# Loading the first x tile by DMA transposes alone, and W1's first blocks from another queue

## The chip, the cores and the metric

The kernel runs on one core of a Trainium2 chip. The metric is the device time of one execution in microseconds (us); lower is better. Times of several executions are given as a median.

## The reference

The kernel computes a gated mix of two branches over a sequence x of 2048 rows and 640 columns, in bf16. Branch a is a state space layer (a linear recurrence with complex coefficients over the rows), branch b is a two-layer perceptron with GELU and 1728 hidden columns.

```
x = A_x
g = sigmoid((x * gate_w).sum(-1, keepdims=True))
# a: S5 layer
dt = exp(log_dt);  Lam_bar = exp(dt * Lam)
B_bar = ((Lam_bar - 1.0) / Lam)[:, None] * Bmat
Bu = einsum("bld,pd->blp", x, B_bar)
h[t] = Lam_bar * h[t-1] + Bu[t]
a = 2.0 * einsum("blp,dp->bld", hseq, Cmat).real + x * Dskip
# b: perceptron
b = gelu(x @ w1 + b1) @ w2 + b2
return g * a + (1 - g) * b
```

## The kernel before

The 2048 rows are worked in four tiles (q = 0 to 3) of 512 rows. The matmuls need x with its columns on the partitions, so each tile is held transposed in `xT[q]`: five slabs (k = 0 to 4) of 128 columns by 512 rows. Most tiles are transposed on the way in by DMA (`xtrans`, a `dma_start_transpose` from DRAM). The first tile is made in two ways. Slabs 0 and 1 are loaded as they lie, in two halves of 256 rows (`xna0`, `xna1`, into `xn[0]`), transposed on TensorE against an identity matrix (L428, four transposes per half), and copied out of PSUM by VectorE (L434). Slabs 2, and 3 and 4, come by two DMA transposes.

The first stage is `m1_first`: the first eight blocks (jf) of 128 hidden columns, for tile 0, one PSUM bank each, summed over the five slabs with the slab as the outer loop, so that each slab and each W1 block (`w1load(k)`, 128 rows of W1 by 1024 columns, 256 KB) is wanted only when its turn comes. In slab 0, six of the eight matmuls are split in two halves of 256 rows, so that the first half can run when only the first half load has come. The matmuls of the last block for slabs 0 and 1 are put off until shortly before it is wanted for slab 2, because its bank (7) is used before that for other things. After `m1_first`, `m1` (L675) works the remaining five blocks of tile 0, bank 0 first, each as one group over the five slabs; bank 0 has to be emptied by ScalarE's first GELU (L662) before that. Then come the projection into the state space (`bproj`, L718), VectorE's recurrence (`ssm`), the second perceptron layer and the output projection.

Ahead of it TensorE runs some matmuls on a constant ("warm", L416) and, between transposes and real matmuls, one filler (L441).

The small vectors (Lambda, log_dt, b1) are loaded as rows of one tile and transposed on TensorE into columns ("cols", L455). VectorE copies them out (L460), and a chain of small steps on ScalarE and VectorE follows: two exponentials, an angle, two sines, each kind with its own ScalarE table load; then the GELU table is loaded, and the GELUs start. VectorE goes on from there to the tables of the recurrence.

The order on each engine is not that of the source. Every operation is given to a list scheduler with an estimated duration, its dependencies and a priority (`prio`); at each step the engine that is free earliest takes its released operation with the lowest priority number. The order so found is emitted as one stream for each engine, with semaphore waits for the dependencies. On SP's stream are most loads; on ScalarE's stream, ahead of all its computing, W1's block 0 and the small rows. TensorE's matmuls are numbered in the order of the source (`pe_prio`), and "cols" has priority 20.5 among them.

Of the kernel before, what the change touches and what calls it, by code (L numbers as in the profile page):

```python
# [147 lines left out]
class Prog:  # L148
# [8 lines left out]
    def op(self, name, eng, dur, reads, writes, fn, prio=None, lat=0.0, after=()):  # L157
        deps = {}
        for k in reads:
            for w in self.last_w.get(k, ()):  # L160
                deps[w.idx] = w
        for k in writes:
            for w in self.last_w.get(k, ()):
                deps[w.idx] = w
            for r in self.last_r.get(k, ()):
                deps[r.idx] = r
        for a in after:
            deps[a.idx] = a
        deps = list(deps.values())
        E = self.E  # L170

        def run(eg, deps=deps, eng=eng, fn=fn):
            E.wait(eng, *[d.done for d in deps if not (eng == "pe" and d.eng == "pe")])
            return fn()

        it = self.sch.add(name, eng, dur, deps, run, prio=prio, lat=lat)
        for k in writes:
            self.last_w[k] = [it]
            self.last_r[k] = []
        for k in reads:  # L180
            self.last_r.setdefault(k, []).append(it)
        return it


def bass_gated_mix__ssm_conv_s5__dense_activation_gelu__prompt_kernel(
# [40 lines left out]
    with ExitStack() as es:  # L226
# [83 lines left out]
        def inc(eng, ins):  # L310
            return E.inc(eng, ins, eng + "_s")

        def dma_inc(eng, ins, sem):
            SEM(sem)
            E.count.setdefault(sem, 0)
            ins.then_inc(sems[sem], 16)
            E.count[sem] += 16
            return (sem, E.count[sem])

        def d_act(n):  # L320
            return 0.26 + n * 0.00084
# [4 lines left out]
        def d_mm(n):  # L326
            return n / 2400.0 + 0.004


        def load(name, eng, sem, dst, src, writes, prio, dur=0.5, lat=2.5, reads=(), after=()):  # L330
            def fn():
                with nc.allow_non_contiguous_dma(reason="columns of small vectors"):
                    return dma_inc(eng, engines[eng].dma_start(dst, src), sem)
            return op(name, eng, dur, reads, writes, fn, prio=prio, lat=lat, after=after)

        def load_T(name, sem, pairs, writes, prio, dur, lat=3.0, reads=()):
            def fn():
                t = None
                for dst, src in pairs:
                    t = dma_inc("sp", nc.sync.dma_start_transpose(dst, src), sem)  # L340
                return t
            return op(name, "sp", dur, reads, writes, fn, prio=prio, lat=lat)

        def xnload(q, eng, prio=None):
            load(f"xn{q}", eng, f"l_xn{q}", xn[q % 2][:, :, :],
# [4 lines left out]
        FW = NW * 128  # L350
        nmain = (NF - 1) * 128

        def xtrans(q, ks, prio, dur):
            load_T(f"xT{q}_{ks[0]}", f"l_xT{q}_{ks[0]}", [(xT[q][:, ks[0]:ks[-1] + 1, :], x2[q * 512:(q + 1) * 512, ks[0] * 128:(ks[-1] + 1) * 128])],
                   [("xT", q, k) for k in ks], prio, dur)

        WSPLIT = {}

# [5 lines left out]
        def w1tok(k, jf):  # L364
            return ("w1", k, int(jf >= WSPLIT.get(k, NW)))

        KN = 2

        for h in range(2):
            load(f"xna{h}", "sp", f"l_xna{h}", xn[0][:, 2 * h:2 * h + 2, 0:KN * 128],  # L370
                 x2[h * 256:(h + 1) * 256, 0:KN * 128].rearrange("(c p) d -> p c d", p=128), [("xna", h)], 0.2 * h, dur=0.45, lat=2.0 + 0.4 * h)
        w1load(1, "sp", 1)
        w1load(2, "sp", 4)
        xtrans(0, range(2, 3), 5, 1.15)
        w1load(3, "sp", 6)
        xtrans(0, range(3, 5), 7, 1.8)
        w1load(4, "sp", 8)
# [8 lines left out]
            return inc("pool", nc.gpsimd.memset(rows[:, :], 0.0))  # L386

        op("rz", "pool", 0.2, (), list(ROWS) + [("b1b", 0), ("b1b", 1), "rz"], f_rz, prio=-90)
        w1load(0, "act", -110, reads=["rz"])
        for i, (nm, (r0, src)) in enumerate(ROWS.items()):  # L390
            src = src.rearrange("(k p) -> k p", p=128)
            load(nm, "act", "l_" + nm, rows[r0:r0 + src.shape[0], :], src, [nm], prio=-100 + i, dur=0.4)
# [19 lines left out]

        def f_warm():
            t = None
            for n in (512,) * 5 + (384,):
                t = nc.tensor.matmul(PS[4][:, 0:n], one.broadcast_to([128, 128]), one.broadcast_to([128, n]), start=True, stop=True)  # L416
            return inc("pe", t)

        op("warm", "pe", 2.7, (), [("bank", 4)], f_warm, prio=-1000)

        for i, (k, c0, c1) in enumerate(((0, 0, 2), (1, 0, 2), (0, 2, 4), (1, 2, 4))):
            bank = (7, 6, 7, 6)[i]
            pt = PS[bank][:, :].bitcast(BF16)[:, 0:(c1 - c0) * 128]

            def f_xt(k=k, pt=pt, c0=c0, c1=c1):
                t = None
                for c in range(c0, c1):
                    t = nc.tensor.transpose(pt[:, (c - c0) * 128:(c - c0 + 1) * 128], xn[0][:, c, k * 128:(k + 1) * 128], ident[:, :])  # L428
                return inc("pe", t)

            op(f"xt{i}", "pe", 0.11 * (c1 - c0), [("xna", c0 // 2), "ident"], [("bank", bank)], f_xt, prio=-990 + i if i < 2 else 3.1 + 0.1 * i)

            def f_xc(k=k, pt=pt, c0=c0, c1=c1):
                return inc("dve", nc.vector.tensor_copy(out=xT[0][:, k, c0 * 128:c1 * 128], in_=pt))  # L434

            op(f"xc{i}", "dve", 0.42, [("bank", bank)], [("xT", 0, k, c0)], f_xc, prio=-2000 + i)

        def f_fill():
            t = None
            for _ in range(1):  # L440
                t = nc.tensor.matmul(PS[3][:, 0:256], one.broadcast_to([128, 128]), one.broadcast_to([128, 256]), start=True, stop=True)  # L441
            return inc("pe", t)

        op("fill", "pe", 0.11, [("xna", 0), "ident"], [("bank", 3)], f_fill, prio=-900)

        XK0 = [[("xT", 0, k)] for k in range(KD)]
        XK0[0] = [("xT", 0, 0, 0), ("xT", 0, 0, 2)]
        XK0[1] = [("xT", 0, 1, 0), ("xT", 0, 1, 2)]
        XT = {q: [("xT", q, k) for k in range(KD)] for q in range(1, NQ)}
        XT[0] = [t for x in XK0 for t in x]  # L450

        psC = PS[7][:, :].bitcast(BF16)[:, 0:128]

        def f_cols():
            return inc("pe", nc.tensor.transpose(psC, rows[:, :], ident[:, :]))  # L455

        op("cols", "pe", 0.3, list(ROWS) + [("b1b", 0), ("b1b", 1), "ident"], [("bank", 7)], f_cols, prio=20.5)

        def f_cols1():
            return inc("dve", nc.vector.tensor_copy(out=cols[:, :], in_=psC[:, 0:RT + 1]))  # L460
# [128 lines left out]
        for ci, src in enumerate((A_B_re, A_B_im)):  # L589
            for i, (p0, p1) in enumerate(((0, 512), (512, KP * 128))):  # L590
                load_T(f"B{ci}{i}", f"l_B{ci}{i}", [(BT[:, ci, :, p0:p1], src[p0:p1, :])], [("BT", ci, i)], prio=30 + ci + 0.1 * i, dur=0.8 * (p1 - p0) / 128)
        xtrans(1, range(KD), 32, 3.4)
        load("gwb", "sp", "l_gwb", gwb[:, :], gate_w.partition_broadcast(128), ["gwb"], prio=32.2)
        load("xnb", "sp", "l_xnb", xn[0][:, :, KN * 128:D], x2[0:512, KN * 128:D].rearrange("(c p) d -> p c d", p=128),
             [("xn", 0, 0), ("xn", 0, 1)], 32.4, dur=1.0, lat=6.0, reads=[("xna", 0), ("xna", 1)])
        big = load("w2a", "sp", "l_w2a", W2sb[:, 0:NF - 1, :], B_w2[0:nmain, :].rearrange("(j p) d -> p j d", p=128), ["w2a"], prio=33, lat=8.0)
        load("w2b", "sp", "l_w2b", W2sb[0:FL, NF - 1, :], B_w2[nmain:F, :], ["w2b"], prio=34, lat=4.0)
        load("w2c", "sp", "l_w2c", W2sb[64:64 + FL, NF - 1, :], B_w2[nmain:F, :], ["w2c"], prio=34.2, lat=4.0)
# [42 lines left out]


        def m1_first():
            late = [(0, NW - 1), (1, NW - 1)]
            seq = [(k, jf) for k in range(KD) for jf in range(NW) if (k, jf) not in late]
            i = seq.index((2, NW - 1))
            seq[i:i] = late
            steps = [(0, jf, h) for h in range(2) for jf in range(6)] + [(k, jf, None) for k, jf in seq if k or jf > 5]
            for k, jf, h in steps:
                t0, t1 = (0, 512) if h is None else (256 * h, 256 * h + 256)  # L650

                def f_mm(jf=jf, k=k, t0=t0, t1=t1):
                    return inc("pe", nc.tensor.matmul(PS[jf][:, t0:t1], W1sb[:, k, jf * 128:(jf + 1) * 128], xT[0][:, k, t0:t1],  # L653
                                                      start=(k == 0 and t0 == 0), stop=(k == KD - 1), skip_group_check=jf < 6))

                op(f"m1_0_{jf}_{k}_{t0}", "pe", d_mm(t1 - t0), (XK0[k] if h is None else XK0[k][h:h + 1]) + [w1tok(k, jf)], [("bank", jf)],
                   f_mm, prio=pe_prio())
            for jf in range(NW):
                ctr["bank"] += 1

                def f_ge(jf=jf):
                    return inc("act", nc.scalar.activation(Gl[0][:, jf, :], PS[jf][:, :], ACT.Gelu_apprx_tanh, bias=b1col[:, jf:jf + 1]))  # L662

                op(f"ge_0_{jf}", "act", d_act(512), [("bank", jf), "b1col"], [("gl", 0, jf)], f_ge, prio=10)
# [344 lines left out]
        def outsT(q, mid=None):  # L1009
# [58 lines left out]
            for d in range(KD):  # L1068

                def f_dx(d=d):  # L1070
                    for _ in range(14 if q == NQ - 2 else 0):
                        nc.scalar.nop(nofuse=True)
                    return inc("act", nc.scalar.activation(xT[q][:, d, :], xT[q][:, d, :], ACT.Copy, scale=cols2[:, 1, d:d + 1]))  # L1073

                op(f"dx_{q}_{d}", "act", d_act(512), [("cols2", 1)], XK0[d] if q == 0 else [("xT", q, d)], f_dx, prio=20)

            for d in range(KD):
                bank = next_bank()
# [123 lines left out]
```

## Time and profile before

| | us |
|---|---|
| median of 3 runs | 212.66 (212.58 to 212.69) |
| the profiled execution | 211.84 |
| its span in the profile | 210.5 |
| TensorE busy | 206.9 (98%) |
| VectorE busy | 191.0 (91%) |
| ScalarE busy | 102.7 (49%) |

The profiled execution's time is 1.34 us more than its span, which counts from the first to the last event of the core. In the timeline a line gives the start, the time from the first start to the last end of the instructions merged in it, the engine, the line of the kernel and the operation; "SPq" and "ACTq" are the issues of transfers from those engines' streams. A transfer's time to landing is counted from its issue. PEld are TensorE's weight loads, which overlap its matmuls. Matmuls overlap one another in the records: a 512-column matmul is recorded as 379 ns long while the next starts earlier.

### The profile page before, as it was taken

Reading aid. Unit: us, or ns where it says so; the run is one execution under the profiler, and the core shown is the slowest. Engines: PE = TensorE matmul, PEld = TensorE weight load, DVE = VectorE, ACT = ScalarE, POOL = GpSimd, SP = SyncE. Lnnn points to the kernel's source line nnn. Section 1 sums busy time; section 2 is a strip of 40 time slices with the busy share of each in tenths; the row PEclk is TensorE's granted clock in tenths of the full one; section 3 lists DMA queues with packets and bytes.
Section 4 is the critical chain, followed back from the end, with each engine's and each line's share of the span. In section 5 each row is a group of like instructions: output and inputs, shape, how many; then the busy total and the mean of one; then the engine's idle time right before and its main releaser. Section 6 shows DMA issues by size and latency. Waiting matters only on the chain.

```text
span 210.5 us, 2557 instructions
## 1 busy us (share of the span) xinstructions
PE 206.9 (98%) x987; PEld 95.1 (45%) x1004; DVE 191.0 (91%) x244; ACT 102.7 (49%) x166; POOL 4.2 (2%) x12
## 2 busy tenths in 40 slices
PE   8999999999999999999999999999999999999996
PEld 4544444444444444444444444444444444444444
DVE  2499999999999999999999999899999999899482
ACT  2398556679850533556683222455664253204321
POOL 1000000030000000000000000000010000000000
DMA  6999999999500020053373000006631000006623
GB/s 191 271 230 124 200 204 226 361 190 207 129 0 4 0 50 0 0 107 65 80 61 113 3 0 0 0 2 140 142 87 58 0 0 4 0 2 145 135 71 100
DMA packets 50248, 19.47 MB, mean 93 GB/s; under 512 B 43068, under 2 KB 48828, under 8 KB 50236
## 3 DMA queue, kind: packets, MB, share of 16 engines
q1 hardware_dynamic: 47904, 17.59, 38.2%
q0 software_dynamic: 1600, 1.32, 4.3%
q10 hardware_dynamic: 732, 0.40, 0.7%
q8 instruction: 8, 0.13, 0.3%
q14 instruction: 4, 0.03, 0.1%
HBM read 8.68 MB, written 2.63 MB: 54 GB/s over the span
## 4 chain that ended last, share of the span: by engine, by line
PE 98%; issue 0%; DVE 0%
PE ps L675 22%; PE ps L718 20%; PE ps L1015 20%; PE ps L1085 15%; PE ps L809 5%; PE ps L653 4%; PE ps L922 4%; PE ps L829 1%; PE ps L416 1%; PE ps L696 1%; PE ps L882 1%; PE ps L1050 1%; PE ps L428 0%; PE ps L846 0%; DVE W1sb L954 0%
## 5 line engine op out<-in xcount | busy, mean ns | idle before, releaser
L675 PE MATMUL ps<-xT,W1sb 128*128 128x512 bf16 x214 | 47.5, 379 | 0.3
L762 DVE TENSOR_TENSOR_SCAN W<-atab,V 128x1280 bf16<-128x1280 f32 x16 | 44.3, 2812 | 0.3
L718 PE MATMUL ps<-xT,BT 128*128 128x512 bf16 x196 | 43.3, 379 | 0.2
L1015 PE MATMUL ps<-Gl,W2sb 128*128 128x512 bf16 x192 | 42.8, 379 | 0.2
L682 ACT ACTIVATE Gl<-ps,cols 128x512 bf16<-128x512 f32 x44 | 29.8, 695 | 15.5 <-PE ps L675 15.5
L675 PEld LDWEIGHTS ps<-xT,W1sb 128*128 128x128 bf16 x220 | 21.5, 98 | 26.0
L1085 PE MATMUL ps<-Hb,CT 128*128 128x512 bf16 x150 | 32.9, 379 | 0.0
L729 ACT ACTIVATE U<-ps 128x512 bf16<-128x512 f32 x40 | 23.7, 596 | 15.5 <-PE ps L718 15.5
L718 PEld LDWEIGHTS ps<-xT,BT 128*128 128x128 bf16 x200 | 19.4, 98 | 23.8 <-ACT Gt L704 0.4
L1015 PEld LDWEIGHTS ps<-Gl,W2sb 128*128 128x128 bf16 x195 | 18.9, 98 | 23.3 <-issue 0.7
L1023 ACT ACTIVATE E1T<-ps,cols 128x512 bf16<-128x512 f32 x15 | 10.0, 686 | 26.2 <-PE ps L1015 14.7
L1085 PEld LDWEIGHTS ps<-Hb,CT 128*128 128x128 bf16 x150 | 14.7, 98 | 17.7
L1093 ACT ACTIVATE E2T<-ps 128x512 bf16<-128x512 f32 x15 | 9.0, 597 | 21.7 <-PE ps L1085 21.7
L627 DVE SCALAR_TENSOR_TENSOR trf<-xn,gwb 128x640 bf16<-128x640 bf16 x16 | 13.2, 823 | 0.4
L505 DVE TENSOR_TENSOR V<-V,W 128x1280 bf16<-128x1280 bf16 x16 | 12.5, 821 | 0.3
L505 DVE TENSOR_TENSOR Hb<-Hb,V 128x1280 bf16<-128x1280 bf16 x16 | 12.5, 821 | 0.3
L505 DVE TENSOR_TENSOR V<-mr,U 128x2560 bf16<-128x2560 bf16 x8 | 11.9, 1492 | 0.3
L505 DVE TENSOR_TENSOR Hb<-c,W 128x2560 bf16<-128x2560 bf16 x8 | 11.9, 1490 | 0.2
L809 PE MATMUL ps<-W2sb,Gl 128*128 128x512 bf16 x51 | 11.8, 379 | 0.1
L505 DVE TENSOR_TENSOR V<-s,W 128x2560 bf16<-128x2560 bf16 x8 | 11.9, 1484 | 0.0
L505 DVE TENSOR_TENSOR W<-mi,U 128x2560 bf16<-128x2560 bf16 x8 | 11.9, 1483 | 0.0
L1073 ACT ACTIVATE xT<-xT,cols 128x512 bf16<-128x512 bf16 x15 | 10.0, 712 | 0.0
(103 smaller groups left out, 148.2 us busy)
## 6 DMA issues: line engine op xcount, KB each, us to landing
W2sb<-in_B_w_dram SPq DMA_DIRECT2D x1, 2080.0 KB, 8.4
out_dram<-xn SPq DMA_DIRECT2D x3, 640.0 KB, 5.5
xn<-in_A_x_dram POOLq DMA_DIRECT2D x2, 640.0 KB, 7.0
W1sb<-in_B_w_dram SPq DMA_DIRECT2D x4, 256.0 KB, 4.0
trf<-grow SPq DMA_DIRECT2D x4, 256.0 KB, 4.9
xn<-in_A_x_dram SPq DMA_DIRECT2D x1, 640.0 KB, 7.2
W1sb<-in_B_w_dram SPq DMA_DIRECT2D x1, 480.0 KB, 5.6
W1sb<-in_B_w_dram SPq DMA_DIRECT2D x1, 400.0 KB, 6.4
```

Of the source, the lines that this page charges most:

```text
L505: return inc("dve", nc.vector.tensor_tensor(out=o, in0=a, in1=b, op=o_))
L627: t = inc("dve", nc.vector.scalar_tensor_tensor(out=scr[:, :], in0=xn[q % 2][:, c, :], scalar=1.0, in1=gwb[:, :], op0=ALU.mult, op1=ALU.mu ...
L675: t = nc.tensor.matmul(PS[bank][:, :], W1sb[:, k, jf * 128:(jf + 1) * 128], xT[q][:, k, :], start=(k == 0), stop=(k == KD - 1))
L682: return inc("act", nc.scalar.activation(Gl[q % 2][:, jf, :], PS[bank][:, :], ACT.Gelu_apprx_tanh, bias=b1col[:, jf:jf + 1]))
L718: t = nc.tensor.matmul(PS[bank][:, :], BT[:, ci, kd, k * 128:(k + 1) * 128], xT[q][:, kd, :], start=(kd == 0), stop=(kd == KD - 1))
L729: return inc("act", nc.scalar.activation(dst, src, ACT.Copy, scale=1.0 if ci == 0 else -1.0))
L762: t = inc("dve", nc.vector.tensor_tensor_scan(out=g[:, ci, :], data0=a, data1=v[:, ci, :], initial=0.0, op0=ALU.mult, op1=ALU.add))
L809: t = nc.tensor.matmul(PS[bank][:, :], Gl[q % 2][:, jf, t4 * 128:(t4 + 1) * 128], W2sb[:, jf, 0:DN], start=False, stop=False, skip_group_c ...
L1015: t = nc.tensor.matmul(PS[bank][:, :], W2sb[:, jf, d * 128:(d + 1) * 128], Gl[q % 2][:, jf, :], start=(jf == 0 and not lead), stop=(jf == ...
L1023: return inc("act", nc.scalar.activation(E1T[:, d, :], PS[bank][:, :], ACT.Identity, bias=cols2[:, 0, d:d + 1]))
L1073: return inc("act", nc.scalar.activation(xT[q][:, d, :], xT[q][:, d, :], ACT.Copy, scale=cols2[:, 1, d:d + 1]))
L1085: t = nc.tensor.matmul(PS[bank][:, :].rearrange("p (s t) -> p s t", s=2), CT[:, ci, k, d * 128:(d + 1) * 128], Hb[:, 2 * (q % 2):2 * (q % ...
```

## The change

The two half loads, the eight TensorE transposes, VectorE's four copies, the filler and the splitting of matmuls go. Slab 0, and slabs 1 and 2, come by two DMA transposes that are the first two transfers of SP's stream. W1's blocks 0, 1 and 2 are issued at the head of ScalarE's stream, without waiting for the clearing of the rows tile, in place of one there and two on SP's. One more constant matmul of 512 columns is in the warming. The priority of "cols" goes from 20.5 to 18.5. Later, `xn[0]` is loaded whole (640 KB) in place of the three slabs that were missing (384 KB).

```
-        KN = 2
-
-        for h in range(2):
-            load(f"xna{h}", "sp", f"l_xna{h}", xn[0][:, 2 * h:2 * h + 2, 0:KN * 128],
-                 x2[h * 256:(h + 1) * 256, 0:KN * 128].rearrange("(c p) d -> p c d", p=128), [("xna", h)], 0.2 * h, dur=0.45, lat=2.0 + 0.4 * h)
-        w1load(1, "sp", 1)
-        w1load(2, "sp", 4)
-        xtrans(0, range(2, 3), 5, 1.15)
+        xtrans(0, range(0, 1), 0, 1.2)
+        xtrans(0, range(1, 3), 1, 1.2)
         w1load(3, "sp", 6)
         xtrans(0, range(3, 5), 7, 1.8)
         w1load(4, "sp", 8)
...
-        w1load(0, "act", -110, reads=["rz"])
+        w1load(0, "act", -110)
+        w1load(1, "act", -109)
+        w1load(2, "act", -108)
...
-            for n in (512,) * 5 + (384,):
+            for n in (512,) * 6 + (384,):
...
-        for i, (k, c0, c1) in enumerate(((0, 0, 2), (1, 0, 2), (0, 2, 4), (1, 2, 4))):
...
-        op("fill", "pe", 0.11, [("xna", 0), "ident"], [("bank", 3)], f_fill, prio=-900)
...
-        op("cols", "pe", 0.3, list(ROWS) + [("b1b", 0), ("b1b", 1), "ident"], [("bank", 7)], f_cols, prio=20.5)
+        op("cols", "pe", 0.3, list(ROWS) + [("b1b", 0), ("b1b", 1), "ident"], [("bank", 7)], f_cols, prio=18.5)
...
-        load("xnb", "sp", "l_xnb", xn[0][:, :, KN * 128:D], x2[0:512, KN * 128:D].rearrange("(c p) d -> p c d", p=128),
-             [("xn", 0, 0), ("xn", 0, 1)], 32.4, dur=1.0, lat=6.0, reads=[("xna", 0), ("xna", 1)])
+        xnload(0, "sp", 32.4)
...
-            late = [(0, NW - 1), (1, NW - 1)]
-            seq = [(k, jf) for k in range(KD) for jf in range(NW) if (k, jf) not in late]
+            seq = [(k, jf) for k in range(KD) for jf in range(NW) if k > 1 or jf < NW - 1]
             i = seq.index((2, NW - 1))
-            seq[i:i] = late
-            steps = [(0, jf, h) for h in range(2) for jf in range(6)] + [(k, jf, None) for k, jf in seq if k or jf > 5]
-            for k, jf, h in steps:
-                t0, t1 = (0, 512) if h is None else (256 * h, 256 * h + 256)
-
-                def f_mm(jf=jf, k=k, t0=t0, t1=t1):
-                    return inc("pe", nc.tensor.matmul(PS[jf][:, t0:t1], W1sb[:, k, jf * 128:(jf + 1) * 128], xT[0][:, k, t0:t1],
-                                                      start=(k == 0 and t0 == 0), stop=(k == KD - 1), skip_group_check=jf < 6))
-
-                op(f"m1_0_{jf}_{k}_{t0}", "pe", d_mm(t1 - t0), (XK0[k] if h is None else XK0[k][h:h + 1]) + [w1tok(k, jf)], [("bank", jf)],
-                   f_mm, prio=pe_prio())
+            seq[i:i] = [(0, NW - 1), (1, NW - 1)]
+            for k, jf in seq:
+
+                def f_mm(jf=jf, k=k):
+                    return inc("pe", nc.tensor.matmul(PS[jf][:, :], W1sb[:, k, jf * 128:(jf + 1) * 128], xT[0][:, k, :],
+                                                      start=(k == 0), stop=(k == KD - 1)))
+
+                op(f"m1_0_{jf}_{k}", "pe", d_mm(512), [("xT", 0, k), w1tok(k, jf)], [("bank", jf)], f_mm, prio=pe_prio())
```

More of the change, by code (lines that the diff above doesn't have):

```diff
@@ L334, in load, with load_T @@
             return op(name, eng, dur, reads, writes, fn, prio=prio, lat=lat, after=after)
-        def load_T(name, sem, pairs, writes, prio, dur, lat=3.0, reads=()):
+        def load_T(name, sem, pairs, writes, prio, dur, lat=3.0, reads=(), eng="sp"):
             def fn():
@@ L339, in fn @@
                 for dst, src in pairs:
-                    t = dma_inc("sp", nc.sync.dma_start_transpose(dst, src), sem)
+                    t = dma_inc(eng, engines[eng].dma_start_transpose(dst, src), sem)
                 return t
-            return op(name, "sp", dur, reads, writes, fn, prio=prio, lat=lat)
+            return op(name, eng, dur, reads, writes, fn, prio=prio, lat=lat)
         def xnload(q, eng, prio=None):
@@ L351, in bass_gated_mix__ssm_conv_s5__dense_activation_gelu__prompt_kernel, with xtrans @@
         nmain = (NF - 1) * 128
-        def xtrans(q, ks, prio, dur):
+        def xtrans(q, ks, prio, dur, eng="sp"):
             load_T(f"xT{q}_{ks[0]}", f"l_xT{q}_{ks[0]}", [(xT[q][:, ks[0]:ks[-1] + 1, :], x2[q * 512:(q + 1) * 512, ks[0] * 128:(ks[-1] + 1) * 128])],
-                   [("xT", q, k) for k in ks], prio, dur)
+                   [("xT", q, k) for k in ks], prio, dur, eng=eng)
         WSPLIT = {}
@@ L419, in bass_gated_mix__ssm_conv_s5__dense_activation_gelu__prompt_kernel @@
         op("warm", "pe", 2.7, (), [("bank", 4)], f_warm, prio=-1000)
-        for i, (k, c0, c1) in enumerate(((0, 0, 2), (1, 0, 2), (0, 2, 4), (1, 2, 4))):
[L422 to L442, printed above, removed]
-        op("fill", "pe", 0.11, [("xna", 0), "ident"], [("bank", 3)], f_fill, prio=-900)
[L446 to L450, printed above, removed]
+        XT = {q: [("xT", q, k) for k in range(KD)] for q in range(NQ)}
         psC = PS[7][:, :].bitcast(BF16)[:, 0:128]
@@ L1073, in f_dx @@
                     return inc("act", nc.scalar.activation(xT[q][:, d, :], xT[q][:, d, :], ACT.Copy, scale=cols2[:, 1, d:d + 1]))
-                op(f"dx_{q}_{d}", "act", d_act(512), [("cols2", 1)], XK0[d] if q == 0 else [("xT", q, d)], f_dx, prio=20)
+                op(f"dx_{q}_{d}", "act", d_act(512), [("cols2", 1)], [("xT", q, d)], f_dx, prio=20)
             for d in range(KD):
```

## The prediction

> **What bounds the kernel now.** I read the page first: engine shares and the chain that ended last.
>
> ```profile
> PE 206.9 (98%) x987; PEld 95.1 (45%) x1004; DVE 191.0 (91%) x244; ACT 102.7 (49%) x166; POOL 4.2 (2%) x12
> PE 98%; issue 0%; DVE 0%
> ```
>
> TensorE is busy nearly all the span and the chain never leaves it. A change at the start is therefore worth what it does to the moment at which TensorE falls into its unbroken stream: all later work slides with it. So I read TensorE's timeline at the start, then the queues' (start, length, what):
>
> ```profile
> 0.78 2.61 PE L416 MATMUL ps<-const-bfloat16-1.0 128*128 128x512 bf16 x6 [0.78 <-PEq L1187]
> 3.19 0.63 PE L428 MATMUL ps<-ident,xn 128*128 128x128 bf16 x4
> 3.61 0.42 PE L441 MATMUL ps<-const-bfloat16-1.0 128*128 128x256 bf16 x1
> 3.99 0.72 PE L653 MATMUL ps<-xT,W1sb 128*128 128x256 bf16 x3
> 4.55 0.39 PE L428 MATMUL ps<-ident,xn 128*128 128x128 bf16 x4
> 4.77 2.99 PE L653 MATMUL ps<-xT,W1sb 128*128 128x256 bf16 x17
> 7.60 0.22 PE L455 MATMUL ps<-ident,rows 128*128 128x128 bf16 x1
> 7.66 5.78 PE L653 MATMUL ps<-xT,W1sb 128*128 128x512 bf16 x25
> 13.27 1.03 PE L675 MATMUL ps<-xT,W1sb 128*128 128x512 bf16 x4
> ...
> 2.74 1.20 SPq L340 DMA_TRANSPOSE xT<-in_A_x_dram  x1
> 4.61 1.25 SPq L340 DMA_TRANSPOSE xT<-in_A_x_dram  x1
> ```
>
> The stream's rate: 25 L675 matmuls run from 13.27 to 18.66, 0.2155 us each. The 40 full matmuls of the first tile take 8.62 us of it, and the transpose of the small rows ("cols", L455) 0.055. Counted back from 13.27, an unbroken stream would have started at **4.60**. The first real matmul is at 3.99, but waits and 8 transposes in between use up the lead. 4.60 is the number to beat.
>
> **What is removed.** Two loads of half of x's first two slabs, 8 TensorE transposes, one filler, 4 VectorE copies, and the splitting of 6 matmuls into 12. All of TensorE's part lies before the stream closes up, so its whole worth is in the 4.60. The copies (0.3 us each) go from an engine that idles 2.4 us just ahead of them: nothing more. An added 512-column warming matmul (0.43 us apart in the trace there) ends the warming at 0.78 + 6 x 0.427 + 0.32 = 3.66, before any data can be there: nothing.
>
> **When the first matmul can start.** It needs slab 0 and W1's block 0. Block 0, now without the wait for the memset, is issued at 0.74 instead of 0.97; its 2.8 us to landing give 3.54. A DMA transpose of one slab from DRAM landed 4.2 us after issue (queued behind 512 KB of W1); one of the same size between SBUF tiles, late in the kernel with idle queues, 2.4:
>
> ```profile
> DMA to landing us min/median/max: 4.2/4.2/4.3
> ...
> DMA to landing us min/median/max: 2.4/2.4/2.4
> ```
>
> (the first answer is for xT in the first 14 us, the second for the transpose into Gl). So slab 0 lands between 0.74 + 2.4 = 3.14 and 0.74 + 4.2 = 4.94. It has an empty queue of its own but three W1 blocks beside it; I take 4.3 (estimate, a little above the middle). Seven matmuls, one of them still at the slow clock, end at about 6.0.
>
> **When the second slab is there.** Block k=1 now waits for the two-slab transpose, issued right behind the first at 0.74 + 1.20 = 1.95. Nearest row: the two-slab transpose of before, 4.3 us, which gives 6.25. Bytes say the same: slab 0, slabs 1 and 2 and W1's three blocks are 1152 KB, exactly what before had moved (half loads, three blocks, slab 2) between the first packet at 1.8 and the last at about 6.25, semaphore at 6.94. My first packets are at about 2.0 (an ACT load showed its own 1.3 us after issue), so at the same pace the last lands at 7.1; were the pieces to run one after the other at their own best rates (about 350 GB/s for W1, 288 for transposes in the trace), at 2.0 + 3.6 + 0.7 = 6.3. Shortest: 3.6 us, the small second B_re transpose, gives 5.6. I take 6.35 and a start of k=1 at 6.4, bounds 5.65 to 7.15. An unbroken stream from 4.60 would start k=1 at 4.60 + 7 x 0.2155 = 6.10. **Term 1: +0.3 us** (-0.45 to +1.05).
>
> The W1 blocks take 0.40 us of issue each on ScalarE's queue; queued behind them are the six loads of the small rows, last issue about 4.1 instead of 3.57, wanted only past 8.5, and ScalarE's first table load, wanted past 9. The Trainium skill ("DMA: Bandwidth & Descriptors", section "Issuing engines are not separate DMA queues") says that transfers from several issuers share the same 16 engines and that spreading them saves issue time only. By that rule, 7.1 stands before 6.3. The trace agrees as far as it goes: while both queues had work (2.2 to 3.6) the total stayed at 290 to 420 GB/s, near one queue's own.
>
> **What the order does to GELU.** This is a wait that the diff hides. "cols" feeds the chain to the first GELU:
>
> ```profile
> 7.86 0.19 DVE L460 CAST cols<-ps 128x29 f32<-128x29 bf16 x1 [2.51 <-PE ps L455]
> 8.82 1.28 ACT L498 ACT_TABLE_LOAD   x1
> 10.76 1.28 ACT L662 ACT_TABLE_LOAD   x1
> 12.06 1.84 ACT L662 ACTIVATE Gl<-ps,cols 128x512 bf16<-128x512 f32 x3
> ```
>
> It is a serial chain: 4.46 us from cols (7.60) to GELU (12.06), 0.69 for the first one, bank 0 free at 12.75. TensorE wants bank 0 at 13.27: 0.52 us of slack. In the order of before, cols stands behind work equal to 14 full matmuls; in the new order (priority 18.5) it stands behind 18. Four matmuls are 0.86 us, so the slack turns into 0.52 - 0.86 = -0.34, plus a semaphore: **term 2: +0.4 us** (0.3 to 0.5; zero only if some later wait on TensorE, say for slabs 3 and 4, holds it anyway). Later banks come free every 0.6 us and are wanted every 1.08, so only the first waits.
>
> **What is moved or grows, at no cost.** W1's block 3 and all behind it on SP's queue are issued about 0.75 us earlier (transposes 1.20 + 1.25 in place of 0.97 + 0.94 + 1.20, and the block): slabs 3 and 4 at 3.85, plus 4.3, land at 8.15, wanted at about 10; the rest of W1 was there at 12.3 and 13.6 for 13.3 and 16.5. The full x load in place of the 384 KB one adds 256 KB, 0.9 us at 290 GB/s, ahead of two x transposes and W2; W2 would land at about 42.7 instead of 41.8 and is first used at 56.66. VectorE's long chain starts relative to TensorE 0.86 - 0.4, about 0.5 us later; the first matmul on its result runs at 71.77, the result is complete at 67.94; at the end VectorE idles 2.7 us at once. Without those covers each would cost its own size.
>
> **Sum.** +0.3 + 0.4 = +0.7 us. The profiled execution is 211.84 (span 210.5 and 1.34 around it), which becomes 212.55; the median of the runs is 212.66, 0.82 more, so I add the same 0.7 to it: **213.4 us**. A change within 0.2%, 0.43 us, can't be told from none here.
>
> **Rivals.**
> (a) The forecast, about 212.9 to 213.9: chance 0.5.
> (b) Not slower: transposes at the head of an empty queue go through nearly as the 2.4 us row. The first matmul starts at 3.6 as W1 allows, one or two run at the slow clock, and k=1 starts at its lower bound 5.65: -0.45, and with cols' wait about -0.05, 212.6. It decides where slabs 1 and 2 land before 5.6. Over 0.43 us faster it is only if the GELU wait is covered too, at 212.2. For it: nothing stands ahead of them. Against: 768 KB of W1 ask the same engines at the same moment, and every DRAM transpose shown took 3.6 or more. Chance 0.25, of that 0.1 clearly faster.
> (c) The transposes get the engines last: 7.1, term 1 is +1.0, sum +1.4, 214.1. For it: from 2.6 to 3.2 of the trace ScalarE's block took nearly all packets while SP's second half load waited. Chance 0.13.
> (d) The clock. Until about 4.4 TensorE runs at half rate: weight loads last 147 ns before and 98 after, 512-column matmuls stand 427 ns apart and later 215.5, though the page's granted clock reads 1.00 throughout. It rises some 3.6 us after the first matmul, having seen near-unbroken work. Now TensorE idles from 3.66 to 4.3. If that delays the rise to 7 or later, seven matmuls take 3.0 us, k=1 starts at 7.3 and some of its own are slow: about +1.1 over the forecast, 214.5. Against: the new warming is 2.88 us of real matmuls, as much as before had without counting transposes. Chance 0.12. The Trainium skill ("TensorE: Matmul & The Clock Gate", Part 1) says the clock is released after a sustained busy window of about 3.4 us, free-running; the rise at 4.4 fits that, and whether 0.6 us idle breaks it no run here shows.
> That the change would not do what it says is out: in the new order the two transposes are SP's first two and the blocks ScalarE's first three, with no wait ahead.
>
> **Range and chances.** 212.4 to 214.6 takes in (b) to (d) but for their ends. Slower by over 0.2% holds (c), (d) and most of (a): 0.65; same 0.24; faster 0.11.
>
> **What would show it.** Right: first real matmul at 4.0 to 4.6, a gap on TensorE ahead of k=1 until about 6.4, released by the DMA into xT, a second gap of 0.3 to 0.5 ahead of the first L637 matmul (the old L675), released by ScalarE's GELU, that matmul at about 14.0. Wrong: no gap at k=1 (b), weight loads of 147 ns past 5 (d), no wait on GELU, or a new TensorE gap anywhere after 20 us.

## The result and the profile after

The changed kernel takes 215.26 us (median of 4 runs, 214.1 to 215.59), the kernel before 212.62 us in the same comparison (4 runs). The ratio is 1.0119, 95% interval 1.0077 to 1.016: about 2.5 us slower, where 0.7 was forecast, and above the stated range. The profiled execution of after took 215.59 us; its span is 214.3, 3.8 longer than that of before.

TensorE's timeline and the queues' at the start of the changed kernel, as shown for before:

```profile
0.74 1.36 ACTq L333 DMA_DIRECT2D W1sb<-in_B_w_dram  x3
0.74 2.56 SPq L340 DMA_TRANSPOSE xT<-in_A_x_dram  x2
...
0.78 3.04 PE L412 MATMUL ps<-const-bfloat16-1.0 128*128 128x512 bf16 x7 [0.78 <-PEq L1149]
5.43 6.21 PE L616 MATMUL ps<-xT,W1sb 128*128 128x512 bf16 x18 [1.61 <-DMA xT<-in_A_x_dram]
11.48 0.22 PE L422 MATMUL ps<-ident,rows 128*128 128x128 bf16 x1
11.53 4.91 PE L616 MATMUL ps<-xT,W1sb 128*128 128x512 bf16 x22
16.77 5.56 PE L637 MATMUL ps<-xT,W1sb 128*128 128x512 bf16 x25 [0.33 <-ACT Gl L624]
```

TensorE idles for 1.61 us until slab 0 lands, its first real matmul is at 5.43 instead of 3.99, and the first L637 matmul (L675 of before) is at 16.77 instead of 13.27: +3.50. From there on the two timelines keep that distance (the first L680 matmul, L718 of before, at 22.16 against 18.66; the last transfers' issue at 211.95 against 208.45). So all of the loss but 0.3 us sits ahead of 16.8 us; the 0.3 comes behind the issue of the last stores. The part ahead of 16.8 us has three pieces that can be read here.

The two transposes' times to landing (first slab 0, then slabs 1 and 2):

```profile
DMA to landing us min/median/max: 4.6/4.6/4.6
...
DMA to landing us min/median/max: 5.7/5.7/5.7
```

They land at 5.34 and about 7.7. The weight loads, one for each matmul, show the clock. First two of the kernel before, then those of L616 in the changed one:

```profile
4.39 0.15 PEld L428 LDWEIGHTS ps<-ident,xn 128*128 128x128 bf16 x1
6.09 0.10 PEld L653 LDWEIGHTS ps<-xT,W1sb 128*128 128x128 bf16 x1
...
5.83 0.15 PEld L616 LDWEIGHTS ps<-xT,W1sb 128*128 128x128 bf16 x1 [0.28 <-issue]
7.96 0.15 PEld L616 LDWEIGHTS ps<-xT,W1sb 128*128 128x128 bf16 x1 [0.28 <-DMA xT<-in_A_x_dram]
9.67 0.15 PEld L616 LDWEIGHTS ps<-xT,W1sb 128*128 128x128 bf16 x1 [0.28 <-issue]
9.97 1.18 PEld L616 LDWEIGHTS ps<-xT,W1sb 128*128 128x128 bf16 x6
```

In the changed kernel they last 147 ns and stand 0.43 us apart until just before 9.97; in the trace of before those of 147 ns end at 4.4. The 18 matmuls from 5.43 to 11.48 take 6.05 us, where at 0.2155 us each they would take 3.88: the slow clock costs 2.17 us. The wait for GELU costs more than the 0.33 us shown: the 22 matmuls behind "cols" start at 11.53 and would, at 0.2155 us each, let L637 start at 16.27, so the stream loses 0.50. (The idle time shown counts from the recorded end of the last matmul, and a matmul recorded as 379 ns long ends 0.16 us after the next could have started.) An unbroken full-speed stream from 5.43 would reach L637 at 5.43 + 8.675 = 14.1; with 2.17 for the clock and 0.50 for GELU this is 16.77, all of it. Against before, the 3.50 us are thus 0.83 for the later start (5.43 against 4.60), 2.17 and 0.50.

There is no gap ahead of k=1: slabs 1 and 2 land at 7.7, and the seven slow matmuls of k=0 end only at about 8.4. So the parts overlap: at full clock TensorE would have stood waiting for slabs 1 and 2 until 7.7. What each is worth alone is a matter for runs.

### The profile page after: what moved, and what is told of

Same layout as the page of the kernel before. It is cut to its first block, busy times and chain, and to the rows that moved or that the text cites. A ratio compares the mean times of both kernels' runs of the same rounds, so it can differ in the third digit from the quotient of the medians.

```text
span 214.3 us, 2540 instructions
## 1 busy us (share of the span) xinstructions
PE 209.4 (98%) x990; PEld 94.3 (44%) x990; DVE 190.0 (89%) x240; ACT 102.7 (48%) x166; POOL 4.2 (2%) x12
## 4 chain that ended last, share of the span: by engine, by line
PE 94%; DMA 2%; ACT 1%; DVE 1%; issue 0%
PE ps L637 22%; PE ps L680 20%; PE ps L977 20%; PE ps L1047 15%; PE ps L771 5%; PE ps L884 4%; PE ps L616 3%; DMA xT<-in_A_x_dram 2%; PE ps L791 1%; PE ps L658 1%; PE ps L844 1%; PE ps L1012 1%; ACT L624 1%; ACT Gl L624 0%; PE ps L808 0%
## 5 line engine op out<-in xcount | busy, mean ns | idle before, releaser
L637 PE MATMUL ps<-xT,W1sb 128*128 128x512 bf16 x220 | 48.1, 379 | 0.3 <-ACT Gl L624 0.3
L680 PE MATMUL ps<-xT,BT 128*128 128x512 bf16 x200 | 43.8, 379 | 0.0
L637 PEld LDWEIGHTS ps<-xT,W1sb 128*128 128x128 bf16 x220 | 21.4, 98 | 26.5 <-issue 0.8
L680 PEld LDWEIGHTS ps<-xT,BT 128*128 128x128 bf16 x200 | 19.4, 98 | 23.8 <-ACT Gt L666 0.4
L616 PE MATMUL ps<-xT,W1sb 128*128 128x512 bf16 x40 | 11.0, 443 | 1.6 <-DMA xT<-in_A_x_dram 1.6
```

The source lines that it names most:

```text
L616: return inc("pe", nc.tensor.matmul(PS[jf][:, :], W1sb[:, k, jf * 128:(jf + 1) * 128], xT[0][:, k, :], start=(k == 0), stop=(k == KD - 1)))
L637: t = nc.tensor.matmul(PS[bank][:, :], W1sb[:, k, jf * 128:(jf + 1) * 128], xT[q][:, k, :], start=(k == 0), stop=(k == KD - 1))
L680: t = nc.tensor.matmul(PS[bank][:, :], BT[:, ci, kd, k * 128:(k + 1) * 128], xT[q][:, kd, :], start=(kd == 0), stop=(kd == KD - 1))
```

## The experiments

Each kernel was timed against the kernel before on the same chip; its median was 212.1 to 212.3 us in these comparisons. Differences in us are worked out from the ratios, which take in all runs of a kernel and can differ by some tenths of a us from the difference of two medians. The kernel before ran at 211.76 to 212.78 us in these comparisons, and its profile is of a run of 211.84, near the fast end; differences between two profiles can therefore be larger than those between all runs.

**A busy TensorE until the data come** (`e1_warm`, on the changed kernel):

```
-            for n in (512,) * 6 + (384,):
+            for n in (512,) * 11 + (384,):
```

> The changed kernel with 11 instead of 6 warming matmuls of 512 columns, so that TensorE has no idle time before slab 0 lands at about 5.4. Theory (the idle time from 3.8 to 5.4 broke the busy stretch that the clock needs): slow weight loads (147 ns) end by about 5 instead of 10, the seven matmuls of k=0 run at 0.2155 us, k=1 then waits for slabs 1 and 2 at about 7.75, and the first L637 matmul comes at 7.75 + 33 x 0.2155 + 0.055 + 0.33 = 15.25 instead of 16.77: about 1.5 us less, 213.7. Rival (the loss is the late landing of the transposes, the slow clock only fills time that would be waited anyway): under 0.3 us less than the changed kernel, about 215.

Measured: 214.06 us, ratio to before 1.0081 (1.0063 to 1.0098). TensorE's timeline:

```profile
0.78 4.53 PE L412 MATMUL ps<-const-bfloat16-1.0 128*128 128x512 bf16 x12 [0.78 <-PEq L1149]
5.24 1.68 PE L616 MATMUL ps<-xT,W1sb 128*128 128x512 bf16 x7
7.91 2.55 PE L616 MATMUL ps<-xT,W1sb 128*128 128x512 bf16 x11 [0.99 <-DMA xT<-in_A_x_dram]
...
15.59 2.75 PE L637 MATMUL ps<-xT,W1sb 128*128 128x512 bf16 x12 [0.32 <-ACT Gl L624]
```

The slow weight loads end at 4.55, the seven matmuls of k=0 take 1.68 us instead of 3, and then TensorE waits for slabs 1 and 2 until 7.91. L637 comes at 15.59, 1.2 us sooner than in after. The idle stretch thus kept the clock low; its net price is 1.2 us in the profiles and, between the two ratios, 0.4% or 0.8 us. The two ratios' intervals overlap (1.0077 to 1.016 and 1.0063 to 1.0098), so the 0.8 is rough. What is left, 1.7 us, is not the clock.

**The clock alone** (`e2_before_idle`, on the kernel before; no transfer is touched):

```
-            for n in (512,) * 5 + (384,):
+            for n in (512,) * 2:
```

> The kernel before with only 2 warming matmuls of 512 columns; no transfer is touched. TensorE idles from about 1.8 to 3.2. Theory (clock): the rise moves from about 4.4 to between 7 and 10.5, some 6 to 14 matmuls run at 0.427 instead of 0.2155 us: 1.3 to 3 us slower, 214 to 215.6. Rival (clock not tied to idle time, or covered by the waits for slabs): within 0.3 us of 212.6.

Measured: 213.05 us, ratio 1.0044 (1.0028 to 1.0061); L675 at 14.74 instead of 13.27. TensorE sits idle for 1.26 us (to 3.05), slow weight loads go on to 7.8 instead of 4.4. The direction is the theory's and the rival is out. The loss is 1.5 us in the profiles; by the ratio it is 0.9, under the expected 1.3 to 3, and the rise, at 7.8, came at the early end of what was expected.

**The GELU wait alone** (`e3_before_cols`, on the kernel before):

```
-        op("cols", ..., [("bank", 7)], f_cols, prio=20.5)
+        op("cols", ..., [("bank", 7)], f_cols, prio=24.5)
```

> The kernel before with the transpose of the small rows four full matmuls later (priority 24.5), nothing else. Theory (the 0.52 us of slack ahead of the first GELU turn into a wait of 0.34 us plus a semaphore): a TensorE wait of 0.3 to 0.4 us ahead of the first L675 matmul, released by GELU, 213.0. Rival (the chain to GELU is covered): no wait, 212.6.

Measured: 212.53 us, ratio 1.0022 (1.001 to 1.0034), 0.5 us. The wait is there, of the size worked out, and as in after it costs the stream more than is shown (22 matmuls from 8.66 would end in a start at 13.40; L675 comes at 13.89, 0.49 later):

```profile
8.61 0.22 PE L455 MATMUL ps<-ident,rows 128*128 128x128 bf16 x1
8.66 4.91 PE L653 MATMUL ps<-xT,W1sb 128*128 128x512 bf16 x21
13.89 4.48 PE L675 MATMUL ps<-xT,W1sb 128*128 128x512 bf16 x20 [0.32 <-ACT Gl L662]
```

**Both taken out of the changed kernel** (`e4_warm_cols`): 11 warming matmuls as in `e1_warm`, and

```
-        op("cols", ..., [("bank", 7)], f_cols, prio=18.5)
+        op("cols", ..., [("bank", 7)], f_cols, prio=14.5)
```

> The changed kernel with 11 warming matmuls (as e1_warm) and the transpose of the small rows after 14 instead of 18 matmuls (priority 14.5). Theory: the wait of 0.32 us for the first GELU goes, and nothing takes its place: first L637 matmul at about 15.25 instead of 15.6, 0.3 us under e1_warm. Rival (another wait, for slabs 3 and 4 or for the small rows, is late next): no gain over e1_warm.

Measured: 213.05 us, ratio 1.0039 (1.0026 to 1.0053). No wait on GELU is left and L637 comes at 14.69:

```profile
7.50 1.69 PE L616 MATMUL ps<-xT,W1sb 128*128 128x512 bf16 x7 [0.47 <-DMA xT<-in_A_x_dram]
```

The step from `e1_warm` is 0.9 us in the profiles: the GELU wait cost the stream of `e1_warm` 0.49, and in this execution slabs 1 and 2 also landed 0.4 us sooner (k=1 at 7.50). What is left against before, 0.8 us by the ratio and 1.42 in the profiles, is the late data: k=1 starts 1.40 us after the 6.10 of an unbroken stream.

**W1's blocks back on SP's queue** (`e5_w1_sp`, on the changed kernel):

```
         xtrans(0, range(0, 1), 0, 1.2)
+        w1load(1, "sp", 0.5)
         xtrans(0, range(1, 3), 1, 1.2)
+        w1load(2, "sp", 4)
...
-        w1load(1, "act", -109)
-        w1load(2, "act", -108)
```

(The planner's assumed latencies of the loads that are moved or stand next to them are lowered as well, so that TensorE's order stays that of after; these arguments are left out of the lines shown here, and in `e7_mix` and `e8_behind`.)

> The changed kernel with W1's blocks 1 and 2 back on SP's queue, block 1 behind the first transpose and block 2 behind the second; block 0 stays on ScalarE's. Theory (slab 0's data had passed by 3.6, and only its last small packets, the completion, stood behind the W1 blocks of ScalarE's queue until 5.3): slab 0 lands at 0.74 + 3.5 = about 4.3, TensorE's first real matmul at 4.3 to 4.5. Rival (a transpose from DRAM at the head of the queue takes 4.6 whatever runs beside it): first matmul at 5.4 again. Time by the theory 213 to 214.3, since slabs 1 and 2 are issued 0.5 later; by the rival 215 or more.

Measured: 213.54 us, ratio 1.0087 (1.0054 to 1.0119); four of its six runs are at 213.4 to 213.6, two at 215.2 and 215.3. Slab 0 lands after 3.6 instead of 4.6 us, slabs 1 and 2 after 4.1 instead of 5.7:

```profile
4.38 2.22 PE L616 MATMUL ps<-xT,W1sb 128*128 128x512 bf16 x7 [0.56 <-DMA xT<-in_A_x_dram]
6.77 1.68 PE L616 MATMUL ps<-xT,W1sb 128*128 128x512 bf16 x7 [0.17 <-DMA xT<-in_A_x_dram]
8.74 1.04 PE L616 MATMUL ps<-xT,W1sb 128*128 128x512 bf16 x4 [0.28 <-DMA W1sb<-in_B_w_dram]
```

The rival, that a DRAM transpose at the head takes 4.6 whatever runs beside it, is out. The packets of the queues in the trace of after (q1 is SP's, q10 ScalarE's; packets, MB, share), first for 2.6 to 3.6 us, then for 3.6 to 4.8, show where the microsecond was:

```profile
q1 hardware_dynamic: 512, 0.13, 57.4%
q10 hardware_dynamic: 102, 0.18, 50.2%
...
q10 hardware_dynamic: 183, 0.34, 106.5%
q1 hardware_dynamic: 34, 0.00, 1.7%
```

Slab 0's 512 rows had all moved by 3.6. In the next 1.2 us SP's queue moved only 34 packets of next to no bytes, among 0.34 MB of ScalarE's queue, and the semaphore came at 5.34. That the 34 are slab 0's completion is an inference; that the W1 blocks on the other queue made it late, the runs show: slab 0 takes 4.6, 4.5 and 4.6 us in the three kernels with all three blocks ahead there (after, `e1_warm`, `e4_warm_cols`) and 3.5 to 4.0 in the four others on the changed kernel.

**That part of the change alone** (`e6_before_act`, on the kernel before):

```
-        w1load(1, "sp", 1)
-        w1load(2, "sp", 4)
...
         w1load(0, "act", -110, reads=["rz"])
+        w1load(1, "act", -109, reads=["rz"])
+        w1load(2, "act", -108, reads=["rz"])
```

> The kernel before with W1's blocks 1 and 2 on ScalarE's queue behind block 0 instead of SP's; nothing else. Theory (transfers from SP complete late when W1 blocks wait on the other queue): the second half load lands at 5 or later instead of 4.1, TensorE waits for it, the first L675 matmul comes 0.5 to 1 us later, 212.6 to 213.1. Rival (the bytes are the same, the place does not matter, and slab 2 is issued 1 us earlier): the same as before or up to 0.2 us less.

Measured: 214.27 us, ratio 1.0097 (1.0082 to 1.0111), 2.1 us. The move of two W1 blocks to the other queue, with nothing else, costs nearly as much as the whole change, above the expected 212.6 to 213.1. The place was not the one expected:

```profile
4.62 3.00 PE L653 MATMUL ps<-xT,W1sb 128*128 128x256 bf16 x17
9.68 0.22 PE L455 MATMUL ps<-ident,rows 128*128 128x128 bf16 x1 [2.06 <-DMA rows<-in_B_b_dram]
9.84 7.46 PE L653 MATMUL ps<-xT,W1sb 128*128 128x512 bf16 x25
17.13 1.24 PE L675 MATMUL ps<-xT,W1sb 128*128 128x512 bf16 x5
```

The second half load landed after 3.1 us instead of 2.9, no matter. Late were the small rows, now behind the two blocks on ScalarE's queue, for which TensorE stood 2.06 us, and slab 2, which took 6.5 us from issue instead of 4.2. Slab 2 was there at 8.3, before the rows, so only the rows held TensorE up; the changed kernel has no such wait, and this run prices the move of the blocks in the kernel before, not their share of the change. After the idle time the clock fell, and here the granted clock shows it (after the engines' busy times: granted clock, DMA share, GB/s):

```profile
10.50:13.80 3.30, 3.30 (x9) 1.17 (x8) 3.08 (x10) 3.02 (x5) 0.00 (x0) 0.50 1.20 323
```

(This profile is the longest of its runs, 215.7; the others were 213.7 to 214.4, which the wait of 2.06 us would account for without the slow matmuls.)

**Only block 1 beside the second transpose** (`e7_mix`, on the changed kernel): 8 warming matmuls, "cols" at 14.5, and

```
         xtrans(0, range(1, 3), 1, 1.2)
+        w1load(2, "sp", 4)
...
-        w1load(1, "act", -109)
-        w1load(2, "act", -108)
+        w1load(1, "act", -98.5)
```

> The changed kernel with W1's block 1 on ScalarE's queue only after two of the small rows, block 2 on SP's behind the two transposes, 8 warming matmuls and the small rows' transpose after 14 matmuls. Theory: slab 0 lands at about 4.4, slabs 1 and 2 at 6.0 to 6.7, no GELU wait, full clock by about 5: the first L637 matmul at 13.3 to 14.0, so 212.1 to 212.9, level with before (212.1 in the last comparison) or up to 0.8 behind. Rival (transposes at the head of the stream always cost some 2 us): 214.

Measured: 213.32 us, ratio 1.0051 (1.0039 to 1.0064). Slab 0 lands after 3.5 us as expected; slabs 1 and 2 take 5.2, k=1 starts at 7.25 and L637 comes at 14.45, so the time is above the expected 212.1 to 212.9. One block on the other queue is enough to hold the second transpose up.

**No further block beside it** (`e8_behind`, on the changed kernel): 8 warming matmuls, "cols" as in after, and blocks 1 and 2 both on SP's queue behind the two transposes:

```
         xtrans(0, range(1, 3), 1, 1.2)
+        w1load(1, "sp", 4)
+        w1load(2, "sp", 5)
...
-        w1load(1, "act", -109)
-        w1load(2, "act", -108)
```

> The changed kernel with W1's blocks 1 and 2 on SP's queue behind both transposes, and 8 warming matmuls. Theory (the second transpose is slow because W1 blocks of the other queue are in flight with it): slabs 1 and 2 land about 4.2 us after issue, near 6.2, instead of 5.4 to 5.8 after; W1's block 1 is then the late one, near 7.3. Rival (behind another transpose from DRAM, a two-slab transpose takes over 5 us by itself): landing at 7.2 or later, with nothing beside it. Time by both near 213.3: the landing decides.

Measured: 213.91 us, ratio 1.0073 (1.0047 to 1.0099). The second transpose's time to landing:

```profile
DMA to landing us min/median/max: 3.7/3.7/3.7
```

3.7 instead of 5.4 to 5.8, so slabs 1 and 2 are there at 5.7, before the 6.10 of an unbroken stream. The rival is out. But now W1's block 1 is late (k=1 at 7.51, released by its load): the same bytes have to come before k=1 in whatever order. They are 896 KB (slabs 0 to 2 and two blocks); the kernel before needs 768 KB for its k=1 (two half loads and two blocks). A transfer of slab 1 alone was not tried.

Are slabs 1 and 2 late because of the queue, or of the bytes alone? With 640 KB issued up to and with them (`e8_behind`) they land at 5.7; with 896 KB at 6.75 and 6.95 where the block stands ahead on SP's own queue (`e5_w1_sp`, `e9_sp_warm`) and at 7.2 where it is on the other one (`e7_mix`); with 1152 KB at 7.45 to 7.9. So, as far as single profiles can tell, most of it goes with the bytes, and for one block 0.25 to 0.45 us with the queue. But the bytes do not pass at an even pace. In the stretch ahead of these landings little moved in after and `e1_warm` (first after, then `e1_warm`; the last column is GB/s):

```profile
5.60:6.40 0.80, 0.80 (x3) 0.29 (x2) 0.00 (x0) 0.26 (x1) 0.00 (x0) 1.00 0.83 96
5.60:6.40 0.80, 0.80 (x6) 0.36 (x4) 0.00 (x0) 0.26 (x1) 0.00 (x0) 1.00 0.25 62
```

In before the same stretch moved 197 GB/s. Why the pace fell stays open.

**The spread of `e5_w1_sp`** (`e9_sp_warm`): that kernel with 8 warming matmuls instead of 6.

> The kernel of e5_w1_sp with 8 instead of 6 warming matmuls. In e5_w1_sp four runs were at 213.4 to 213.6 and two at 215.2 to 215.3. Theory (the two are executions in which the idle time of 0.6 us ahead of slab 0 fell so that the clock rose one window later): with no idle time all runs are at 213.0 to 213.6. Rival (the spread comes from the transfers): runs near 215 stay, about one in three.

Measured: 213.62 us, ratio 1.0066 (1.0051 to 1.008), all six runs at 213.6 to 213.85. The runs at 215.2 are gone, as the theory has it, though six runs are few: were one run in three near 215, none in six would still come up 9 times in 100. The rest did not become shorter, since in its profile too the slow weight loads went on to about 6.1, with no idle time ahead of them; the moment of the rise thus varies by itself as well.

No order tried here beats the kernel before.

## Why the prediction was wrong

**Step that failed: term 1, when slabs 1 and 2 are there.** It was put at +0.3 us, with k=1 starting at 6.4 and 7.15 at the latest. In the changed kernel k=1 started at about 8.4, held by a late slab 0 (5.43) and seven matmuls at the slow clock; slabs 1 and 2, there at 7.7, were past the bound too. At full clock k=1 started at 7.91 and 7.50 (`e1_warm`, `e4_warm_cols`): +1.8 and +1.4 against 6.10, outside the bounds. The nearest row, the two-slab transpose of before with 4.3 us, was taken from a moment when ScalarE's queue held no W1 block. With one or two blocks beside it besides block 0, the same form takes 5.2 to 5.8 us; with block 0 alone, 3.7 (`e8_behind`). The byte count, 7.1, was the better guide and still short, because it took over the pace of before, and that was not kept: 96 GB/s in after from 5.6 to 6.4, 197 in before. The rule of the Trainium skill that was set beside it ("DMA: Bandwidth & Descriptors", section "Issuing engines are not separate DMA queues"), that spreading over issuers saves issue time only, fits in its first half, shared engines: with both queues at work from 2.4 to 4.0 us, after moved 305 to 366 GB/s in all, about what before did (348 and 322). It gives no hint of a loss, and `e6_before_act` measures one of 2.1 us for a spread alone, from the small rows that stood behind the blocks.

**The first matmul.** 4.3 was taken, 5.43 came; the upper bound, 4.94 for the landing, was passed by 0.4. Its cause is the W1 blocks beside it, shown by `e5_w1_sp` and `e7_mix`, which bring the time to landing back to 3.6 and 3.5 us. The transpose's packets also began later than the 2.0 assumed: all 512 of slab 0 fall between 2.6 and 3.6. The lower bound was a single record: the transpose between SBUF tiles that took 2.4 us in before took 4.2 in the profile of after.

**The clock.** Rival (d) had the mechanism and the size nearly right (price 1.1; in the profiles 1.2, by the ratios 0.8) and was given 0.12. That the sizes meet is partly luck: (d) priced some seven slow matmuls, but eleven weight loads were slow at a cost of 2.17 us, of which about half was hidden behind the wait for slabs 1 and 2. The error was to weigh it for an idle time of 0.6 us, which follows from the wrong 4.3, while 1.6 us came. For an idle time of 0.6 us itself the low weight is not contradicted: in the profile of `e5_w1_sp`, with 0.56 us, the rise came at 5.5. Whether it came later in its runs at 215.2 and 215.3 is not shown. Rivals (c), (d) and the start of TensorE were treated as separate cases; one cause, the late transposes, brings all three at once. The rule on a busy window ("TensorE: Matmul & The Clock Gate", Part 1 of the Trainium skill) agrees with the runs: the rise came at about 10 after 1.6 us of idle time and at 4.6 without it, and at 7.8 after 1.26 us in `e2_before_idle`, 4.4 to 4.7 us after work set in again; that the window runs freely fits the rise at 6.1 in `e9_sp_warm`, with no idle time at all.

**Term 2, the GELU wait.** +0.4 was forecast; the wait shown is 0.33 us in after and 0.32 in `e3_before_cols`, and costs the stream 0.50 and 0.49; the time of `e3_before_cols` grew by 0.5 (0.2 to 0.7). The step held, in place and, at the upper end of its 0.3 to 0.5, in size.

**What was costed at nothing.** The later transfers, VectorE's start and the larger x load indeed cost nothing up to the last issue: from 16.8 us on the distance between the timelines is constant. The small rows, "wanted only past 8.5", had less room than it seemed: in `e6_before_act` they came only for 9.68, while in `e4_warm_cols` "cols" ran at 9.02 without a wait for them.

**The sum.** By the ratios: clock 0.8, GELU wait and a slab landing that varies 0.9, late data in the rest 0.8; together the 2.5 measured. These are the steps from one kernel to the next (after, `e1_warm`, `e4_warm_cols`, before), so they add up by construction, and in another order each could be larger or smaller.

## What to carry to other kernels

A transfer's time to landing belongs to what was in flight beside it: before a row is carried over, look at which other queue was loaded at that moment and how many bytes stood ahead, above all where a change moves large loads to another queue. Where a wait at the start of a matmul stream grows, price the clock with it: idle time that looks like 1 us costs the slow matmuls after it as well. And follow small operations through a change of order: the transpose of the small rows, moved four matmuls back, delayed a chain on two other engines and came back as a loss of 0.5 us on TensorE.

## What the runs showed of the hardware

A transfer's data and its semaphore can lie far apart: slab 0's packets had passed by 3.6 us and the wait ended at 5.34 while another queue moved W1 blocks, against 4.3 to 4.8 in the kernels with fewer blocks there. Moving 512 KB of plain loads from one queue to another, bytes unchanged, cost 2.1 us at the start of the kernel, through the small loads behind them. The profiles differ by when TensorE's clock rises: at about 4 to 6.1 us where it had at most 0.6 us of idle time ahead, at 7.8 after 1.26 us, at about 10 after 1.61. At the start the granted clock column reads 1.00 even so; the length of the weight loads, 147 or 98 ns, tells it. Later the column does show a slow stretch (0.50 from 10.5 to 13.8 us in `e6_before_act`).
